# The last tile pair of a down projection: two tiles side by side, or one after the other

## The chip, the core and the metric

The kernel runs on one core of a Trainium2 chip. The core has a matrix engine (TensorE; PE in the profile, its weight loads PEld), a vector engine (VectorE, DVE), a scalar engine (ScalarE, ACT), GpSimd (POOL), and SyncE (SP), which here issues transfers. Matmuls write into PSUM, eight banks of 512 f32 columns each; everything else lives in SBUF, which has 128 partitions. The metric is the time of one execution on the device in microseconds (us), less is better.

## The reference

One row block of 2048 tokens with 640 features, x, goes through two branches that a gate mixes:

```
g = sigmoid((x * gate_w).sum(-1))
a = linear_attention(x) @ wo                     # 32 heads of 20, softmax feature maps
b = (gelu(x @ w_gate) * (x @ w_up)) @ w_down     # 640 -> 1728 -> 640
out = g * a + (1 - g) * b
```

Inputs and output are bf16. The change lies in the last step, where `@ w_down` and `@ wo` are computed and mixed, and in the hidden columns that `@ w_down` reads.

## The kernel before

The 2048 tokens are 16 tiles of 128 rows (t = 0 to 15), in four row blocks (b = 0 to 3) of four tiles. The work goes in this order:

- Attention state (to about 81 us): projections, feature maps and the sums over all tokens.
- Gate and up (`gateup`, to about 195 us): for each block b, 14 chunks c of the 1728 hidden columns, in the order 0, 1, 13, 2, ..., 12. A chunk has 128 columns; the last, c = 13, has 64. For a full chunk TensorE makes five matmuls for the gate into one PSUM bank and five for up into another, ScalarE does the Gelu from the first (line 779) and VectorE multiplies it with the second into `hT`, the hidden activations with hidden columns on partitions (line 781). Chunks take turns on the bank pairs (0, 1) and (6, 7), so a chunk's first matmul waits until the chunk two before it has been read. For c = 13, gate and up fit side by side into 128 columns, so five matmuls into one bank do for both; ScalarE does the Gelu of 64 partitions (line 787), and VectorE multiplies twice (line 792), once for each row half r of `hT` (partitions 0 to 63 and 64 to 127). For block 3, `hT` lies in the space of `xT`, the transposed x, whose first three blocks are done with.
- Down (`downs` and `down_pair`, to the end): tiles go in pairs t0, t0 + 1. Each output element is a sum over 14 chunks of `hT` times `wd_sb` and 5 chunks of `goT` (the attention output, already scaled so that one factor serves both branches) times `wo_sb`. `goT` of tiles 2 to 15 comes from `num`, called between the steps of the pairs ahead (line 968; tiles 14 and 15 during the pair of tiles 12 and 13); it ends in a transposing transfer that SP issues (line 869).

`down_pair` works with matmuls that use 64 of the 128 rows, so that two run side by side, one in each row half, into two banks. A pair is cut into parts h, by output columns: (320, 320), and (256, 256, 128) for the last pair (line 965). In part h, bank `banks[h][j]` holds the columns of tile t0 + j. In the opening, row half r works on bank r: 19 steps of two matmuls (13 full chunks, the half chunk 13, and 5 of `wo_sb`). In the closing, the row halves change banks: 18 steps, because the half chunk has only 64 rows and is needed once for each bank. So in chunk 13 row half r only meets tiles of parity r, and line 792 computes just these: `odd` picks two of the block's four tiles, 64x256 elements for each half.

All parts open first, hidden chunks of every part and then `wo_sb` of every part; then the parts close one after the other. When a part has closed, `evac` multiplies its two banks by the gate's factor into `outsb`: on ScalarE (line 911), and in the last pair the second bank on VectorE (line 909). In the last pair each part's columns of both tiles are then sent to the output in a transfer of their own (line 922); in other pairs there is one transfer at the end. `finish` lets SP wait for all engines and transfers; that is the end of the program.

The helper `_Sched.op` puts a wait in front of an instruction for every earlier one that it depends on (a bank's last reader, a tile's writer). An engine takes its instructions strictly in the order in which the code issues them.

Of the kernel before, what the change touches and what calls it, by code (L numbers as in the profile page):

```python
# [3 lines left out]
P = 128  # L4
# [103 lines left out]
class _Kernel:  # L108
    S, D, H, DH, F = 2048, 640, 32, 20, 1728
    KD = D // P  # L110
# [4 lines left out]
    NFC = 14  # L115
# [644 lines left out]
    def gateup(self, b, c, banks):  # L760
        sc = self.sc
        xs = lambda kt: self.xT[:, kt, b * self.BT:(b + 1) * self.BT]
        xr = [("xT", t) for t in range(4 * b, 4 * b + 4)]
        old = (self.oldw, self.oldk, self.oldq, [("xT", t) for t in range(12)])[b]
        hT, hk = self.hT(b, c), b
        slot = self.gn % 3
        self.gn += 1
        if c < 13:
            i = 0 if c < 7 else 1
            early = c in self.UP + self.LATE  # L770
            done = early and b == 0
            if done:
                banks = banks[::-1]
            for w, wk, bk in ((self.wg_sb, "wg", banks[0]), (self.wu_sb, "wu", banks[1]))[:1 if done else 2]:
                for kt in range(self.KD):
                    key = self.upheld(c)[1] if early and wk == "wu" else (wk, i, kt)
                    self.mm(bk, 0, 512, w[:, kt, c * P:(c + 1) * P], xs(kt), kt == 0, kt == self.KD - 1, xr + [key])
            up, upk = (self.upheld(c)[0], ("upf", c)) if done else (self.bank(banks[1]), ("ps", banks[1]))
            sc.op("act", lambda e: e.activation(self.gl[:, slot, :], self.bank(banks[0]), AF.Gelu_apprx_tanh),  # L779
                  reads=[("ps", banks[0])], writes=[("gl", slot)], guard=self.oldw)  # L780
            sc.op("dve", lambda e: e.tensor_tensor(hT, up, self.gl[:, slot, :], ALU.mult),  # L781
                  reads=[upk, ("gl", slot)], writes=[("hT", hk, c)], guard=old)
        else:
            bk = banks[0]
            for kt in range(self.KD):
                self.mm(bk, 0, 512, self.wgu_sb[:, kt, :], xs(kt), kt == 0, kt == self.KD - 1, xr + ["wgu0", "wgu1"])
            sc.op("act", lambda e: e.activation(self.gl[64:128, slot, :], self.ps[0:64, bk * 512:bk * 512 + 512],
                                                AF.Gelu_apprx_tanh),
                  reads=[("ps", bk)], writes=[("gl", slot)], guard=self.oldw)
            for r in (0, 1):  # L790
                odd = lambda v: v.rearrange("p (u r q) -> p u r q", r=2, q=P)[:, :, r, :]
                sc.op("dve", lambda e: e.tensor_tensor(
                    odd(hT[64 * r:64 * r + 64, :]), odd(self.ps[64:128, bk * 512:bk * 512 + 512]),
                    odd(self.gl[64:128, slot, :]), ALU.mult),
                    reads=[("ps", bk), ("gl", slot)], writes=[("hT", hk, c, r)], guard=old)
# [78 lines left out]
                f()  # L874
        return [lambda p=p: run(p) for p in (small, wide, fin)]

    def down_pair(self, t0, banks, widths):

        sc = self.sc
        ts = (t0, t0 + 1)  # L880
        NFC, KD = self.NFC - 1, self.KD
        nw = len(widths)
        hk = t0 // 4
        last = t0 + 2 == self.NT
        os_ = t0 % 4

        def mm(r, j, h, c, opens, x, n):
            t = ts[j]
            tt, gs, bk, w0, a = t % 4, t % 8, banks[h][j], sum(widths[:h]), 64 * r
            w, end = widths[h], x == n - 1  # L890
            if c <= NFC:
                lhs, rhs = self.hT(hk, c)[a:a + 64, tt * P:(tt + 1) * P], self.wd_sb[a:a + 64, c, w0:w0 + w]
                rd = [("hT", hk, c), "wd"] if c < NFC else [("hT", hk, 13, r), ("wd13", r)]
            else:
                k = c - NFC - 1
                lhs, rhs = self.goT[a:a + 64, gs, k, :], self.wo_sb[a:a + 64, k, w0:w0 + w]
                rd = [("goT", gs), "wo"]
            sc.op("pe", lambda e: e.matmul(self.bank(bk, w), lhs, rhs, start=opens and x == 0, stop=end and not opens,  # L898
                                           skip_group_check=True),
                  reads=rd, writes=[("ps", bk)] + ([("turn", bk)] if end else []), signal=end,  # L900
                  after=[("turn", bk)] if x == 0 and not opens else ())

        def evac(h):
            w0, w = sum(widths[:h]), widths[h]
            for j in (0, 1):
                bk, dst, g = banks[h][j], self.outsb[:, os_ + j, w0:w0 + w], self.Gm[:, ts[j]:ts[j] + 1]
                rd, wr = [("ps", bk), "Gm"], [("outsb", os_ + j, h)]
                if last and j == 1:
                    sc.op("dve", lambda e: e.tensor_scalar(dst, self.bank(bk, w), g, None, op0=ALU.mult), reads=rd, writes=wr)
                else:  # L910
                    sc.op("act", lambda e: e.activation(dst, self.bank(bk, w), AF.Copy, scale=g), reads=rd, writes=wr)  # L911
            if last:
                hs, c0, c1 = [h], w0, w0 + w
            elif h == nw - 1:
                hs, c0, c1 = range(nw), 0, self.D
            else:
                return
            if t0 < self.TB:
                rows = self.out[0:self.BT, :].rearrange("(p j) n -> p j n", j=self.TB)[:, t0:t0 + 2, :]
            else:  # L920
                rows = self.out[t0 * P:(t0 + 2) * P, :].rearrange("(j p) n -> p j n", p=P)
            sc.dma("sp", lambda e: e.dma_start(rows[:, :, c0:c1], self.outsb[:, os_:os_ + 2, c0:c1]),
                   reads=[("outsb", os_ + j, k) for j in (0, 1) for k in hs], writes=[("out", t0, h)])

        wos = [NFC + 1 + k for k in range(KD)]
        opening = list(range(NFC + 1)) + wos
        for part in (range(NFC + 1), range(NFC + 1, len(opening))):
            for h in range(nw):
                for x in part:
                    for r in (0, 1):  # L930
                        mm(r, r, h, opening[x], True, x, len(opening))
                    yield None
        closing = list(range(NFC)) + wos
        for h in range(nw):
            for x, c in enumerate(closing):
                for r in (0, 1):
                    mm(r, 1 - r, h, c, False, x, len(closing))
                if c == closing[-1]:
                    evac(h)
                yield None  # L940
# [8 lines left out]
    def ffn(self):  # L949
        self.gn = 0  # L950
        self.pn = 0
        pairs = [(0, 1), (6, 7)]

        def gateups(b, after, other={}):
            for idx, c in enumerate([0, 1, 13] + list(range(2, 13))):
                self.gateup(b, c, other.get(idx, pairs[self.pn % 2]))
                self.pn += 1
                after(idx)

        def downs(b, side):  # L960
            p = [pairs[(self.pn + k) % 2] for k in (0, 1)]
            n = 0
            for t in (4 * b, 4 * b + 2):
                final = t + 2 == self.NT
                for _ in self.down_pair(t, p + [(2, 3)] if final else p, (256, 256, 128) if final else (320, 320)):
                    n += 1
                    if n in side:
                        self.num(side[n])

        def state(idx):  # L970
            if idx < 4:
                self.gram(12 + idx)
            if idx == 3:
                self.kv_state()
                self.gates()

        left = []

        def first_nums(idx):
            if idx == 4:  # L980
                left.extend(f for steps in self.num_pair() for f in steps)
            for _ in range({4: 1, 5: 1, 6: 2, 7: 1, 8: 1}.get(idx, 0)):
                left.pop(0)()

        def none(idx):
            pass
        at = (1, 31, 61, 91)
        gateups(0, state)
        gateups(1, first_nums, {k: ((0, 1), (0, 1), (0, 5), (1, 2))[k - 5 if k < 7 else 2 + (k - 7) % 2]
                                for k in range(5, 14)})  # L990
        gateups(2, none)
        gateups(3, none)
        for b in range(self.NB):
            downs(b, {at[k]: 4 * b + 2 + k for k in range(4 if b < 3 else 2)})
# [44 lines left out]
```

## Time and profile before

| what | us |
|---|---|
| three runs | 283.30, 283.51, 283.77 (median 283.51) |
| span of the profiled execution, first to last instruction | 282.4 |
| TensorE busy / VectorE / ScalarE | 278.6 / 173.2 / 105.9 |
| attention state, 0 to 81.3: TensorE busy | 79.6 |
| gate and up, 81.3 to 194.8: TensorE busy | 113.5 |
| down without the last pair, 194.8 to 270.0: TensorE busy | 75.2 |
| last pair, 270.0 to 280.3: TensorE busy | 10.3 |
| after the last matmul, 280.3 to 282.4: TensorE busy | 0 |

The granted clock of TensorE is 1.00 in all of these stretches. "Busy" counts a matmul from its start to its modelled end; matmuls overlap in the pipeline, so the pace of a row of matmuls is read from the start of one group to the start of the next, not from the length of a single one. In the timeline a row gives the start, the length, the engine, the line, what is written and read, the shape, and in brackets the idle time before it and what ended that. A matmul's shape is rows used * weight columns, then rows x columns that stream through.

### The profile page before, as it was taken

What the parts mean: (1) busy time and instruction counts of PE and PEld (TensorE: products, weight loads), DVE (VectorE), ACT (ScalarE), POOL (GpSimd) and SP (SyncE); (2) the same over time, 40 slices, a digit from 0 to 9 for tenths busy, and PEclk for the clock granted to TensorE, in tenths of its full rate; (3) what the DMA queues carried; (4) which work ended last, traced back from release to release, by engine and by line L of the source; (5) the groups of instructions that cost most, each with busy time, mean ns of one, the idle gap of its engine ahead of it and who ended that gap; (6) DMA issues with size and microseconds to landing.
All of it is one profiled execution on the core that took longest, in us unless ns stands there. A gap on an engine that the chain in (4) does not pass through costs nothing.

```text
span 282.4 us, 6904 instructions
## 1 busy us (share of the span) xinstructions
PE 278.6 (99%) x2926; PEld 168.6 (60%) x2926; DVE 173.2 (61%) x329; ACT 105.9 (38%) x204; POOL 15.1 (5%) x69
## 2 busy tenths in 40 slices
PE   7999999999999999999999999999999999999996
PEld 4566766665665444444444444445777777777786
DVE  1456999999997523694333324235883883883801
ACT  3246978777793332223232232321112112112011
POOL 7511001101000000000000000000000000000000
PEclk9999999999999999999999999999999999999999
DMA  7999169787789910011000000000133132532221
GB/s 213 193 223 190 29 127 172 153 175 149 157 175 274 350 51 0 2 24 23 2 0 0 0 2 0 0 0 2 26 50 98 46 49 78 66 49 73 73 72 49
DMA packets 60378, 24.11 MB, mean 85 GB/s; under 512 B 51002, under 2 KB 59834, under 8 KB 60346
## 3 DMA queue, kind: packets, MB, share of 16 engines
q1 hardware_dynamic: 59680, 23.63, 38.9%
q8 instruction: 23, 0.38, 0.6%
q10 hardware_dynamic: 666, 0.03, 0.2%
q14 instruction: 9, 0.07, 0.1%
HBM read 9.04 MB, written 2.62 MB: 41 GB/s over the span
## 4 chain that ended last, share of the span: by engine, by line
PE 97%; DMA 1%; SPq 0%; ACT 0%; issue 0%
PE ps L464 58%; PE ps L898 29%; PE ps L599 4%; PE ps L817 2%; PE ps L478 2%; PE ps L637 2%; DMA w<-in_A_wqkv_dram 1%; PE ps L404 1%; SPq L230 0%; SPq L251 0%; ACT outsb L911 0%; PE ps L370 0%
## 5 line engine op out<-in xcount | busy, mean ns | idle before, releaser
L464 PE MATMUL ps<-xT,wu_sb 128*128 128x512 bf16 x260 | 64.1, 379 | 0.0
L464 PE MATMUL ps<-xT,wg_sb 128*128 128x512 bf16 x260 | 63.9, 379 | 0.0
L779 ACT ACTIVATE gl<-ps 128x512 bf16<-128x512 f32 x52 | 31.0, 597 | 70.3 <-PE ps L464 70.3
L464 PE MATMUL ps<-w,xT 128*128 128x362 bf16 (+5 forms) x340 | 51.4, 302 | 0.0
L898 PE MATMUL ps<-wd_sb,hT 64*128 64x320 bf16 x648 | 48.4, 296 | 0.0
L781 DVE TENSOR_TENSOR hT<-ps,gl 128x512 bf16<-128x512 f32 x34 | 23.4, 689 | 37.7 <-PE ps L464 37.7
L464 PEld LDWEIGHTS ps<-xT,wu_sb 128*128 128x128 bf16 x260 | 25.4, 98 | 30.3 <-DVE hT L781 0.2
L464 PEld LDWEIGHTS ps<-xT,wg_sb 128*128 128x128 bf16 x260 | 25.1, 98 | 29.8 <-issue 0.2
L911 ACT ACTIVATE outsb<-ps,Gm 128x320 bf16<-128x320 f32 (+2 forms) x31 | 14.5, 515 | 71.8 <-PE ps L898 71.8
L464 PEld LDWEIGHTS ps<-w,xT 128*128 128x128 bf16 x340 | 31.9, 97 | 14.8
L898 PEld LDWEIGHTS ps<-wd_sb,hT 64*128 64x128 bf16 x648 | 30.9, 94 | 12.2 <-issue 0.4
L898 PE MATMUL ps<-wo_sb,goT 64*128 64x320 bf16 (+2 forms) x340 | 26.5, 288 | 0.0
L617 DVE TENSOR_REDUCE Dk<-Ek 128x66 f32<-128x1320 bf16 x16 | 24.3, 1520 | 2.3 <-ACT gcol L528 2.3
L626 DVE TENSOR_TENSOR Ek<-Ek,Dk 128x1320 bf16<-128x1320 bf16 x16 | 24.5, 1532 | 0.5
L863 DVE TENSOR_TENSOR O<-ps,RH 128x640 bf16<-128x640 f32 x32 | 24.7, 815 | 0.0
L538 ACT ACTIVATE Ek<-ps 128x627 bf16<-128x627 f32 x32 | 20.5, 693 | 6.4 <-PE ps L599 4.9
L538 ACT ACTIVATE Eqt<-ps 128x627 bf16<-128x627 f32 x32 | 20.6, 705 | 2.5 <-PE ps L464 2.5
L781 DVE TENSOR_TENSOR xT<-ps,gl 128x512 bf16<-128x512 f32 x13 | 9.0, 690 | 18.2 <-PE ps L464 18.2
L898 PEld LDWEIGHTS ps<-wo_sb,goT 64*128 64x128 bf16 x340 | 15.9, 94 | 5.3
L898 PE MATMUL ps<-wd_sb,xT 64*128 64x320 bf16 (+2 forms) x270 | 16.0, 269 | 0.0
L851 DVE RECIPROCAL RH<-ps 128x32 f32<-128x32 f32 x16 | 5.7, 357 | 14.4 <-PE ps L817 14.3
L898 PEld LDWEIGHTS ps<-wd_sb,xT 64*128 64x128 bf16 x270 | 12.1, 94 | 2.7
(90 smaller groups left out, 184.1 us busy)
## 6 DMA issues: line engine op xcount, KB each, us to landing
out_dram<-outsb SPq DMA_DIRECT2D x7, 320.0 KB, 2.3
wd_sb<-in_B_w_down_dram SPq DMA_DIRECT2D x1, 2080.0 KB, 11.0
wg_sb<-in_B_w_gate_dram SPq DMA_DIRECT2D x5, 224.0 KB, 3.1
wg_sb<-in_B_w_gate_dram SPq DMA_DIRECT2D x5, 192.0 KB, 3.5
wu_sb<-in_B_w_up_dram SPq DMA_DIRECT2D x5, 192.0 KB, 3.9
wo_sb<-in_A_wo_dram SPq DMA_DIRECT2D x1, 800.0 KB, 9.7
xtok<-in_A_x_dram SPq DMA_DIRECT2D x2, 320.0 KB, 3.3
w<-in_A_wqkv_dram SPq DMA_DIRECT2D x4, 160.0 KB, 4.0
```

The source lines that it names most:

```text
L464: self.sc.op("pe", lambda e: e.matmul(self.ps[:, bank * 512 + c0:bank * 512 + c0 + n], lhs, rhs, start=first, stop=fin), reads=reads, writ ...
L478: sc.op("pe", lambda e, c0=c0, n=n, bk=bk, col=col: e.matmul(self.bank(bk)[:, col:col + n], self.xT[:, kt, t * P:(t + 1) * P], self.w3[:, ...
L538: self.sc.op("act", lambda e: e.activation(dst, src, AF.Exp, scale=scale), reads=[("ps", b), ("ps", b + 1)], writes=[(name, sl, s)])
L599: self.sc.op("pe", lambda e: e.matmul(out, self.xT[:, kt, t * P:(t + 1) * P], self.w3[:, kt, c:c + 2 * n].rearrange("p (r w) -> p r w", w= ...
L617: self.sc.op("dve", lambda e: e.tensor_reduce(self.Dk[:, se, 0, :].rearrange("p (u h) -> p u h", h=self.HG), self.k_view(se), AX.X, ALU.ad ...
L626: sc.op("dve", lambda e: e.tensor_tensor(v, v, R.rearrange("p (u h) -> p u h", h=self.HG).unsqueeze(3).to_broadcast([P, 2 * self.G, self.H ...
L779: sc.op("act", lambda e: e.activation(self.gl[:, slot, :], self.bank(banks[0]), AF.Gelu_apprx_tanh), reads=[("ps", banks[0])], writes=[("g ...
L781: sc.op("dve", lambda e: e.tensor_tensor(hT, up, self.gl[:, slot, :], ALU.mult), reads=[upk, ("gl", slot)], writes=[("hT", hk, c)], guard=old)
L851: dve(lambda e: e.reciprocal(R(0), Dn[1]), rb, [key(0)], guard=old)
L863: dve(lambda e, o=o, f=f, s=s: e.tensor_tensor(o, V[s][:, :, 0:DH], f, ALU.mult), rb + [key(6 + s)], [("O", s, sl)], guard=old)
L898: sc.op("pe", lambda e: e.matmul(self.bank(bk, w), lhs, rhs, start=opens and x == 0, stop=end and not opens, skip_group_check=True), reads ...
L911: sc.op("act", lambda e: e.activation(dst, self.bank(bk, w), AF.Copy, scale=g), reads=rd, writes=wr)
```

## The change

In the last pair both row halves work on columns of the same tile. Part 0 is tile 14: columns 0 to 319 in one bank, 320 to 639 in the other. Part 1 is tile 15, columns 0 to 223 and 224 to 447; part 2 is tile 15, columns 448 to 543 and 544 to 639. The number of matmuls and the columns that they stream in all are the same. Each part goes out in one transfer of one tile: 640, 448 and 192 columns in 128 rows, where there were 256, 256 and 128 columns of two tiles in 256 rows. As each row half now meets both tiles with chunk 13, line 792 computes, for block 3, all four tiles in each row half: two multiplies of 64x512. The other pairs and blocks are as they were.

```diff
@@ -788,7 +788,7 @@
                                                 AF.Gelu_apprx_tanh),
                   reads=[("ps", bk)], writes=[("gl", slot)], guard=self.oldw)
             for r in (0, 1):
-                odd = lambda v: v.rearrange("p (u r q) -> p u r q", r=2, q=P)[:, :, r, :]
+                odd = lambda v: v if b == 3 else v.rearrange("p (u r q) -> p u r q", r=2, q=P)[:, :, r, :]
                 sc.op("dve", lambda e: e.tensor_tensor(
                     odd(hT[64 * r:64 * r + 64, :]), odd(self.ps[64:128, bk * 512:bk * 512 + 512]),
                     odd(self.gl[64:128, slot, :]), ALU.mult),
@@ -874,20 +874,22 @@
                 f()
         return [lambda p=p: run(p) for p in (small, wide, fin)]
 
-    def down_pair(self, t0, banks, widths):
+    def down_pair(self, t0, banks, last):
 
         sc = self.sc
-        ts = (t0, t0 + 1)
-        NFC, KD = self.NFC - 1, self.KD
-        nw = len(widths)
+        NFC, KD, D = self.NFC - 1, self.KD, self.D
         hk = t0 // 4
-        last = t0 + 2 == self.NT
-        os_ = t0 % 4
+        if last:
+            parts = [((t0, 0, 320), (t0, 320, 320)), ((t0 + 1, 0, 224), (t0 + 1, 224, 224)),
+                     ((t0 + 1, 448, 96), (t0 + 1, 544, 96))]
+        else:
+            parts = [((t0, c, 320), (t0 + 1, c, 320)) for c in (0, 320)]
+        nw = len(parts)
 
         def mm(r, j, h, c, opens, x, n):
-            t = ts[j]
-            tt, gs, bk, w0, a = t % 4, t % 8, banks[h][j], sum(widths[:h]), 64 * r
-            w, end = widths[h], x == n - 1
+            t, w0, w = parts[h][j]
+            tt, gs, bk, a = t % 4, t % 8, banks[h][j], 64 * r
+            end = x == n - 1
             if c <= NFC:
                 lhs, rhs = self.hT(hk, c)[a:a + 64, tt * P:(tt + 1) * P], self.wd_sb[a:a + 64, c, w0:w0 + w]
                 rd = [("hT", hk, c), "wd"] if c < NFC else [("hT", hk, 13, r), ("wd13", r)]
@@ -901,26 +903,27 @@
                   after=[("turn", bk)] if x == 0 and not opens else ())
 
         def evac(h):
-            w0, w = sum(widths[:h]), widths[h]
             for j in (0, 1):
-                bk, dst, g = banks[h][j], self.outsb[:, os_ + j, w0:w0 + w], self.Gm[:, ts[j]:ts[j] + 1]
-                rd, wr = [("ps", bk), "Gm"], [("outsb", os_ + j, h)]
+                t, w0, w = parts[h][j]
+                bk, dst, g = banks[h][j], self.outsb[:, t % 4, w0:w0 + w], self.Gm[:, t:t + 1]
+                rd, wr = [("ps", bk), "Gm"], [("outsb", t % 4, h, j)]
                 if last and j == 1:
                     sc.op("dve", lambda e: e.tensor_scalar(dst, self.bank(bk, w), g, None, op0=ALU.mult), reads=rd, writes=wr)
                 else:
                     sc.op("act", lambda e: e.activation(dst, self.bank(bk, w), AF.Copy, scale=g), reads=rd, writes=wr)
+            os_ = t0 % 4
             if last:
-                hs, c0, c1 = [h], w0, w0 + w
+                c1 = w0 + w
+                c0 = parts[h][0][1]
+                sc.dma("sp", lambda e: e.dma_start(self.out[t * P:(t + 1) * P, c0:c1], self.outsb[:, t % 4, c0:c1]),
+                       reads=[("outsb", t % 4, h, j) for j in (0, 1)], writes=[("out", t0, h)])
             elif h == nw - 1:
-                hs, c0, c1 = range(nw), 0, self.D
-            else:
-                return
-            if t0 < self.TB:
-                rows = self.out[0:self.BT, :].rearrange("(p j) n -> p j n", j=self.TB)[:, t0:t0 + 2, :]
-            else:
-                rows = self.out[t0 * P:(t0 + 2) * P, :].rearrange("(j p) n -> p j n", p=P)
-            sc.dma("sp", lambda e: e.dma_start(rows[:, :, c0:c1], self.outsb[:, os_:os_ + 2, c0:c1]),
-                   reads=[("outsb", os_ + j, k) for j in (0, 1) for k in hs], writes=[("out", t0, h)])
+                if t0 < self.TB:
+                    rows = self.out[0:self.BT, :].rearrange("(p j) n -> p j n", j=self.TB)[:, t0:t0 + 2, :]
+                else:
+                    rows = self.out[t0 * P:(t0 + 2) * P, :].rearrange("(j p) n -> p j n", p=P)
+                sc.dma("sp", lambda e: e.dma_start(rows[:, :, :], self.outsb[:, os_:os_ + 2, :]),
+                       reads=[("outsb", os_ + j, k, j) for j in (0, 1) for k in range(nw)], writes=[("out", t0, h)])
 
         wos = [NFC + 1 + k for k in range(KD)]
         opening = list(range(NFC + 1)) + wos
@@ -962,7 +965,7 @@
             n = 0
             for t in (4 * b, 4 * b + 2):
                 final = t + 2 == self.NT
-                for _ in self.down_pair(t, p + [(2, 3)] if final else p, (256, 256, 128) if final else (320, 320)):
+                for _ in self.down_pair(t, p + [(2, 3)] if final else p, final):
                     n += 1
                     if n in side:
                         self.num(side[n])
```

## The prediction

> **What bounds the kernel now.** I read the page's busy table and chain of waits first, then the timeline of the last 12 us, then the timeline of the one other place that the diff touches.
>
> ```profile
> PE 278.6 (99%) x2926; PEld 168.6 (60%) x2926; DVE 173.2 (61%) x329; ACT 105.9 (38%) x204; POOL 15.1 (5%) x69
> ...
> PE 97%; DMA 1%; SPq 0%; ACT 0%; issue 0%
> PE ps L464 58%; PE ps L898 29%; PE ps L599 4%; PE ps L817 2%; PE ps L478 2%; PE ps L637 2%; DMA w<-in_A_wqkv_dram 1%; PE ps L404 1%; SPq L230 0%; SPq L251 0%; ACT outsb L911 0%; PE ps L370 0%
> ```
>
> TensorE is busy 99% of the span and the chain is TensorE for 97%. So a column more or less on TensorE, a wait put in front of it, and the tail behind its last matmul count; nothing else does. The end, from the timeline (start, length, engine, line):
>
> ```profile
> 265.10 1.93 PE L898 MATMUL ps<-wd_sb,xT 64*128 64x320 bf16 x26
> 266.87 0.84 PE L898 MATMUL ps<-wo_sb,goT 64*128 64x320 bf16 x10
> ...
> 271.25 9.88 SPq L922 DMA_DIRECT2D out_dram<-outsb  x4
> ...
> 275.20 1.58 PE L898 MATMUL ps<-wd_sb,xT 64*128 64x256 bf16 x26
> 276.62 0.71 PE L898 MATMUL ps<-wo_sb,goT 64*128 64x256 bf16 x10
> ...
> 279.13 0.89 PE L898 MATMUL ps<-wd_sb,xT 64*128 64x128 bf16 x26
> 279.33 0.48 DVE L909 TENSOR_SCALAR outsb<-ps,Gm 128x256 bf16<-128x256 f32 x1 [1.48 <-PE ps L898]
> 279.86 0.44 PE L898 MATMUL ps<-wo_sb,goT 64*128 64x128 bf16 x10
> 280.37 0.37 ACT L911 ACTIVATE outsb<-ps,Gm 128x128 bf16<-128x128 f32 x1 [0.53 <-PE ps L898]
> ```
>
> The last matmul ends at 279.86 + 0.44 = 280.30; the last evacuation runs from 280.37 to 280.74; the last issue ends at 271.25 + 9.88 = 281.13, and an issue takes 0.37, so it began at 280.76; its transfer lands 1.6 later (its row is shown below), at 282.4, the end of the span. The runs' median, 283.51, lies 1.1 us above this span, and I carry that 1.1 over unchanged.
>
> The other place is the half chunk c = 13 of the last row block, whose two multiplies (line 792) the first hunk of the diff touches:
>
> ```profile
> 170.96 1.24 PE L464 MATMUL ps<-xT,wg_sb 128*128 128x512 bf16 x5
> 171.16 0.59 ACT L787 ACTIVATE gl<-ps 64x512 bf16<-64x512 f32 x1 [1.56 <-PE ps L464]
> 171.85 0.89 DVE L792 TENSOR_TENSOR xT<-ps,gl 64x256 bf16<-64x256 f32 x2 [1.08 <-ACT gl L787]
> 172.04 1.24 PE L464 MATMUL ps<-xT,wu_sb 128*128 128x512 bf16 x5
> 172.91 0.53 PEld L464 LDWEIGHTS ps<-xT,wg_sb 128*128 128x128 bf16 x3
> 173.12 0.59 PE L464 MATMUL ps<-xT,wg_sb 128*128 128x512 bf16 x2
> ```
>
> Chunk 13 has five matmuls and one bank, and only the ten matmuls of c = 2 (170.96 to 173.12) stand between it and c = 3, whose first matmul writes that same bank. VectorE lets go of it at 171.85 + 0.89 = 172.74, and c = 3's first weights load at 172.91: a slack of 0.17 us.
>
> **1. The two wider multiplies at c = 13.** Each row half now needs chunk 13 for all four tiles of the block, so each multiply is 64x512 in place of 64x256. The same kind of operation by shape:
>
> ```profile
> L792 DVE TENSOR_TENSOR xT<-ps,gl x2: 426/428/429, 171.9 to 172.3; 64x256 bf16<-64x256 f32 x2
> ...
> L781 DVE TENSOR_TENSOR xT<-ps,gl x13: 690/690/691, 167.9 to 194.9; 128x512 bf16<-128x512 f32 x13
> ```
>
> Twice the columns cost 0.262 us more. That the partition count doesn't matter I take from ScalarE, where a 64x512 Gelu takes 0.59 (above) and a 128x512 one 0.60 (597 ns on the page). So 0.69 each. They end at 171.85 + 2 x 0.69 + 0.03 (the gap in 0.89 = 2 x 0.428 + 0.03) = 173.26, which is after the 172.91 at which TensorE wants the bank. Its restart: VectorE, idle, began 0.10 after the Gelu ended (171.75 to 171.85), which I take for the release; and from weights to matmul an idle TensorE needs 0.03, as after the gap at 81.27:
>
> ```profile
> 81.27 0.34 PEld L464 LDWEIGHTS ps<-xT,wg_sb 128*128 128x128 bf16 x3 [0.19 <-issue]
> 81.30 0.59 PE L464 MATMUL ps<-xT,wg_sb 128*128 128x512 bf16 x2
> ```
>
> c = 3 then starts at 173.39 in place of 173.12: **+0.27 us**. Behind it in TensorE's queue stands everything that is left, back to back, so nothing gives the stall back. ScalarE and VectorE have about 1.5 us idle ahead of each Gelu and multiply (the 1.56 above), so they only shift along; c = 2's own multiply (173.32 before) finds VectorE free at 173.26. Bounds: at 0.43 a multiply (if the columns cost nothing) there is no stall; at 0.86 (twice the narrow one) they end at 173.60 and the stall is 0.61. A restart of 0.17 + 0.21 (the unstalled distances above) in place of 0.13 gives 0.52.
>
> **2. TensorE in the last pair.** Instructions: three parts, each with 19 opening and 18 closing steps of two matmuls, before and after. Per part, columns go from 256, 256, 128 to 320, 224, 96: the sum stays 640. What can change is the price of a narrow step. Two row halves run side by side; a step of two by start-to-start times: 320 wide (266.87 - 265.10) / 13 = 136 ns; 256 wide (276.62 - 275.20) / 13 = 109 ns; 128 wide (279.86 - 279.13) / 13 = 56 ns; 66 wide, from line 817's matmuls, which also go in row halves:
>
> ```profile
> 263.81 0.50 PE L817 MATMUL ps<-KV,Eq 64*128 64x66 bf16 x22
> 264.15 1.11 PE L898 MATMUL ps<-wo_sb,goT 64*128 64x320 bf16 x14
> ```
>
> (264.15 - 263.81) / 11 = 31 ns. Between these lines, 224 costs 96 and 96 costs 43. New sum 136 + 96 + 43 = 275 ns, old 109 + 109 + 56 = 274; times 37 steps, **+0.04 us**, which is nothing. Bounds: by strict proportion from 128 the 96-wide step is 42 (no gain); if it can't go below the 128-wide 56 ns, it costs 37 x 13 = 0.48 us more. Row 817 at 31 ns speaks for the first.
>
> [...]
>
> Waits: the second part's opening starts later (14 x 136 in place of 14 x 109 ns after the first), which gives the banks it waits for more time; the order of weights, goT and closing is unchanged, and the two goT transposes are issued before the pair begins.
>
> **3. The tail.** The last evacuation is 96 wide in place of 128. ScalarE takes 0.367 for 128 and 0.473 for 256, so 0.83 ns a column: **-0.03**. The last transfer is 48 KB in 128 rows in place of 64 KB in 256:
>
> ```profile
> out_dram<-outsb SPq DMA_DIRECT2D x7, 320.0 KB, 2.3
> ...
> out_dram<-outsb SPq DMA_DIRECT2D x2, 128.0 KB, 1.8
> ...
> out_dram<-outsb SPq DMA_DIRECT2D x1, 64.0 KB, 1.6
> ```
>
> Bytes: (1.8 - 1.6) / 64 x 16 = 0.05 less. Rows: tile pair 2 and 3, also 320 KB but in 128 rows, lands in 2.2 where the 256-row ones take 2.3: 0.1 less. Together -0.15; bounds 0 (landing is a fixed time) and -0.2. I take **-0.12**. The cover for the transfer before it: the second part's evacuation (224 wide, 0.45) starts 18 x 43 = 0.77 before the last matmul's end, so SP has issued that transfer 0.03 + 0.45 + 0.05 + 0.37 = 0.90 after that start, while the last evacuation ends at 0.77 + 0.03 + 0.34 = 1.14. SP keeps 0.24 to spare; without it the end would move by the same amount.
>
> Sum: 0.27 + 0.04 - 0.03 - 0.12 = +0.16, so **283.7 us** on the median, a change of 0.06%. About 0.2% (0.57 us) is what a measurement of this kernel can tell from no change: its runs span 283.30 to 283.77.
>
> **The rivals.**
> A, the forecast: a short stall and a shorter tail that nearly cancel, 283.7. For it: 0.69 against a slack of 0.17. Chance 0.50.
> B, no stall: VectorE treats the now contiguous 64x512 faster, or the release comes in time. Only step 3 is left, 283.51 - 0.15 = 283.4. Against it: all 47 rows of line 781 that read PSUM, contiguous ones, take 0.68 to 0.69. Chance 0.17.
> C, the 96-wide steps are held at the 128-wide pace: +0.16 + 0.44 = 284.1, slower. The place is the third part, opening and closing; it decides from a step above 55 ns. Against it: row 817. Chance 0.11.
> D, the last transfer gets no shorter (its landing is a fixed time, so the parts don't do what they say at the end): +0.28, 283.8. Against it: the three landing times above. Chance 0.12.
> E, the stall is at its upper bound, 0.61, and more where TensorE's weights refill late: 283.51 + 0.61 - 0.11 = 284.0, slower by 0.18%; it passes 284.08 only with D. Chance 0.07.
> Faster by over 0.57 us needs something that no row shows: 0.03.
>
> **How the numbers follow.** Within 0.2% lie A, B, D and most of E; slower is C's better half and a part of E, plus the spread of the runs (0.24 either way around the median): 0.15. Faster, with B's lower end and the spread, 0.06; so 0.79 within. The range 283.2 to 284.1 takes B's 283.4 less 0.2 at one end and C's and E's 284.0 to 284.1 at the other.
>
> **What would show it.** Step 1: in the profile after, line 792 has 64x512 at 0.69 and TensorE shows a gap of about 0.3 us ahead of c = 3, near 173.1, with VectorE named as the releaser; wrong if c = 3 still starts 2.16 us after c = 2. Step 2: 37 steps of the third part at 43 ns; C if at 56. Step 3: the last transfer lands about 1.5 us after its issue, and SP is free before the last evacuation ends. A change beyond 0.6 us either way would make the whole account wrong.

## The result, and the profile after

The changed kernel takes 284.07 us (median of 10 runs, 283.52 to 284.62) where the kernel before, run beside it, takes 283.32 (283.04 to 283.78): a ratio of 1.0022, 95% interval 1.0012 to 1.0032. By the ratio that is +0.62 us, and 0.34 to 0.91 by its interval; the two medians lie 0.75 apart. The forecast was +0.16 with a range of 283.2 to 284.1: the time lies in the range, 0.03 below its upper end, and the sign is right, but the size is nearly four times what was forecast and lies just on the far side of the 0.2% that I had called "within". It also just passes the 0.6 us that the prediction named as the sign that its whole account is wrong; what of the account failed is worked out below.

Before and after can't be compared by absolute times alone, because the start of the program varies from execution to execution (c = 13 of block 3 starts at 169.89 in the profile before, at 169.57 after, though nothing ahead of it was changed). So I measure from that chunk's first matmul, in two lengths:

| profiled execution | c = 13 to the last matmul's end | from there to the end of the program (the tail) | together |
|---|---|---|---|
| before | 110.41 | 2.14 | 112.55 |
| after | 110.71 | 2.60 | 113.31 |
| difference | +0.30 | +0.46 | +0.76 |

The page of the changed kernel, its busy table and its chain of waits by engine and by line:

```profile
PE 277.9 (98%) x2912; PEld 168.0 (59%) x2926; DVE 173.8 (61%) x329; ACT 106.0 (37%) x204; POOL 15.2 (5%) x69
...
PE 96%; DMA 1%; DVE 0%; issue 0%; SPq 0%; ACT 0%; DVEq 0%
PE ps L464 57%; PE ps L900 29%; PE ps L599 4%; PE ps L817 2%; PE ps L478 2%; PE ps L637 2%; DMA w<-in_A_wqkv_dram 1%; PE ps L404 1%; DVE xT L792 0%; SPq L230 0%; ACT gl L787 0%; SPq L251 0%; ACT outsb L913 0%; PE ps L370 0%; DVEq L42 0%
```

TensorE still makes up the chain, but the two multiplies of line 792 and the Gelu of line 787 ahead of them are on it now, which they were not before. (The view infers this chain; for another execution of the changed kernel, e7 below, with the same stall, it leaves them out. The times below are the firmer sign.)

The first term, in the timeline of the changed kernel around c = 13 (start, length, engine, line; in brackets the idle time and what ended it):

```profile
170.85 0.59 ACT L787 ACTIVATE gl<-ps 64x512 bf16<-64x512 f32 x1 [1.56 <-PE ps L464]
171.54 1.42 DVE L792 TENSOR_TENSOR xT<-ps,gl 64x512 bf16<-64x512 f32 x2 [1.08 <-ACT gl L787]
171.73 1.24 PE L464 MATMUL ps<-xT,wu_sb 128*128 128x512 bf16 x5
...
173.08 0.77 PEld L464 LDWEIGHTS ps<-xT,wg_sb 128*128 128x128 bf16 x5 [0.60 <-ACT gl L779]
173.11 1.24 PE L464 MATMUL ps<-xT,wg_sb 128*128 128x512 bf16 x5
```

The two multiplies now end at 171.54 + 1.42 = 172.96; c = 3's weights load 0.12 later and its matmuls start at 173.11. c = 2's last five matmuls start at 171.73; before, c = 3 followed such a start by 173.12 - 172.04 = 1.08, now by 1.38: a stall of 0.30. The view names the Gelu of c = 2 as what ended this wait; but that was done at 172.53. TensorE's queue holds a second wait ahead of this load, for VectorE, and the trace has that one ending at 173.05, 0.09 after the second multiply.

The second term, in the timeline of the end, and in the rows of issues of the transfers view:

```profile
279.35 0.72 PE L900 MATMUL ps<-wd_sb,xT 64*128 64x96 bf16 x26
...
279.90 0.38 PE L900 MATMUL ps<-wo_sb,goT 64*128 64x96 bf16 x10
280.08 1.32 SPq L918 DMA_DIRECT2D out_dram<-outsb  x2
280.32 0.32 DVE L911 TENSOR_SCALAR outsb<-ps,Gm 128x96 bf16<-128x96 f32 x1 [0.32 <-PE ps L900]
280.35 0.34 ACT L913 ACTIVATE outsb<-ps,Gm 128x96 bf16<-128x96 f32 x1 [0.32 <-PE ps L900]
```

```profile
q1 hardware_dynamic: 432, 0.33, 17.1%
q8 instruction: 1, 0.02, 1.6%
issues: line engine op xcount, KB each, median us to landing
out_dram<-outsb SPq DMA_DIRECT2D x1, 160.0 KB, 3.9
out_dram<-outsb SPq DMA_DIRECT2D x1, 112.0 KB, 2.6
out_dram<-outsb SPq DMA_DIRECT2D x1, 48.0 KB, 2.1
```

The 96-wide steps run at (279.90 - 279.35) / 13 = 42 ns, and the last matmul ends at 280.28, 10.31 after the pair's first, as before (269.99 to 280.30). But SP's last issue takes 0.68 (280.72 to 281.40) in place of 0.37, and all three transfers land late: part 0, with half the bytes of a usual pair, takes 3.9 us where a usual pair takes 2.3, and the last takes 2.1 with 48 KB where 64 KB took 1.6. The row above the issues, in the stretch from 278 to 284, is new to this account: one instruction transfer. It holds 1.6% of 16 engines for 6 us, that is 1.5 us on one of them. The trace's packet records put it at 279.53 to 281.02: a single packet of 16 KB. The trace has 16 increments of a semaphore for the landing of each of the three transfers, as many as the page counts DMA engines; I take one increment for one engine's share, 8 of 128 packets. Part 0's transfer has 15 of them by 280.27, and the sixteenth at 282.33. Of its 128 packets 120 are done by 279.90; the last eight, by that reading one DMA engine's share, start only at 281.01, as the fetch ends. The trace doesn't name the engine of a packet; that the fetch and these eight share one is read from these times. (The profile after lacks 14 of the 2926 matmul records; that changes no reading here.)

### The profile page after: what moved, and what is told of

It reads as the page before. It is cut to its first block, busy times and chain, and to the rows that moved or that the text cites. A ratio compares the mean times of both kernels' runs of the same rounds, so it can differ in the third digit from the quotient of the medians.

```text
span 282.9 us, 6888 instructions
## 1 busy us (share of the span) xinstructions
PE 277.9 (98%) x2912; PEld 168.0 (59%) x2926; DVE 173.8 (61%) x329; ACT 106.0 (37%) x204; POOL 15.2 (5%) x69
## 4 chain that ended last, share of the span: by engine, by line
PE 96%; DMA 1%; DVE 0%; issue 0%; SPq 0%; ACT 0%; DVEq 0%
PE ps L464 57%; PE ps L900 29%; PE ps L599 4%; PE ps L817 2%; PE ps L478 2%; PE ps L637 2%; DMA w<-in_A_wqkv_dram 1%; PE ps L404 1%; DVE xT L792 0%; SPq L230 0%; ACT gl L787 0%; SPq L251 0%; ACT outsb L913 0%; PE ps L370 0%; DVEq L42 0%
## 5 line engine op out<-in xcount | busy, mean ns | idle before, releaser
L464 PE MATMUL ps<-xT,wu_sb 128*128 128x512 bf16 x256 | 63.2, 379 | 0.3
L464 PE MATMUL ps<-xT,wg_sb 128*128 128x512 bf16 x250 | 61.8, 379 | 0.7 <-issue 0.2
```

Of the source, the lines that this page charges most:

```text
L464: self.sc.op("pe", lambda e: e.matmul(self.ps[:, bank * 512 + c0:bank * 512 + c0 + n], lhs, rhs, start=first, stop=fin), reads=reads, writ ...
```

## The experiments

Two theories had to be told apart from rivals: S, the stall at c = 13, 0.30 us that nothing gives back; and F, that the last 16 KB fetch of TensorE's instructions holds one DMA engine while part 0's transfer is on it, so that what follows on that engine is late. Ratios are to the kernel before, run on the same chip beside them.

**e1, the wider multiplies alone**, in the kernel before:

```diff
-                odd = lambda v: v.rearrange("p (u r q) -> p u r q", r=2, q=P)[:, :, r, :]
+                odd = lambda v: v if b == 3 else v.rearrange("p (u r q) -> p u r q", r=2, q=P)[:, :, r, :]
```

> The kernel before with only the wider multiplies at c = 13 of block 3 (the extra half is computed and never read). Theory S (stall): TensorE starts c = 3 of block 3 about 0.30 us late, as it did after the change (431 to 432 ns between two starts where a missing record lies, 515 there), and the time is 0.30 us (0.1%) above before; the tail stays as before, with the last transfer landing 1.6 us after its issue. Rival (all of the loss lies in the tail): the gap is given back later, and the time is that of before within 0.1 us.

Measured: 1.0012 (0.9998 to 1.0026), that is +0.34 us, with no change just inside the interval. The profile is sharper: from c = 13 to the last matmul 110.71 (+0.30), tail 2.14 (as before). Its timeline:

```profile
171.51 1.42 DVE L792 TENSOR_TENSOR xT<-ps,gl 64x512 bf16<-64x512 f32 x2 [1.08 <-ACT gl L787]
171.70 1.24 PE L464 MATMUL ps<-xT,wu_sb 128*128 128x512 bf16 x5
...
173.08 1.24 PE L464 MATMUL ps<-xT,wg_sb 128*128 128x512 bf16 x5
```

The same 1.38 between the two starts, from this edit alone. S stands, and the stall is not given back later.

**e2, c = 13 of block 3 in a bank of its own**, in the changed kernel:

```diff
-        gateups(3, none)
+        gateups(3, none, {2: (2, 3)})
```

> The changed kernel with c = 13 of block 3 in bank 2, which nobody uses in that stage, so that c = 3 need not wait for the two multiplies. Theory S: the 0.30 us stall is gone and the time falls by 0.3 us against the changed kernel, to about 0.4 us above before; the last transfer still lands 2 us or more after its issue in most executions. Rival: another wait takes its place (bank 2 is first used again in the down phase), no gain.

Measured: 1.0014 (0.9999 to 1.0028), against 1.0022 for the changed kernel. The two intervals overlap, so the times alone don't show the expected 0.3; the profile does. In it c = 13 to the last matmul is 110.41, exactly as before, with the same 1.42 us of multiplies (c = 3 starts 1.08 after c = 2's last five matmuls again); no other wait took the stall's place. The tail stays at 2.57. This time the fetch came later (279.76 to 281.00), missed part 0 (1.9) and met part 1:

```profile
out_dram<-outsb SPq DMA_DIRECT2D x1, 160.0 KB, 1.9
out_dram<-outsb SPq DMA_DIRECT2D x1, 112.0 KB, 2.4
out_dram<-outsb SPq DMA_DIRECT2D x1, 48.0 KB, 2.1
```

**e3 and e4, the fetch moved out of the way.** The trace has 23 fetches of 16 KB, on average one every 127 matmuls with their weight loads, so I take them for fetches of TensorE's instructions, at about a fixed place in its stream: in the profiles before and after, each of the 23 begins after the same number of weight loads to within 21, the last after 2900 and after 2902 of the 2926. With 56 more matmuls in the warm-up it falls earlier (in e3 it ended 3.35 us ahead of the last issue, in the changed kernel 0.31 after that issue had begun); e3 is the changed kernel, e4 the kernel before with the same edit:

```diff
-        for n in (512, 512, 512, 512, 512, 512, 128, 128, 128):
+        for n in (512, 512, 128, 128, 128):
...
+        for i in range(60):
+            a, b = ((0, 2), (64, 3))[i % 2]
+            sc.op("pe", lambda e: e.matmul(self.bank(b, 16), ones[a:a + 64, 0:P], ones[a:a + 64, 0:16], start=True, stop=True),
+                  writes=[("ps", b)], signal=i >= 60 - 2)
```

> The changed kernel with 56 more matmuls in TensorE's warm-up (60 matmuls of 16 columns in place of 4 of 512), so that the last 16 KB instruction fetch, which comes at a fixed place in TensorE's instruction stream, falls some 2.5 us earlier, about 277 us, ahead of the first of the last three transfers. Theory F (the fetch holds one DMA engine, and the packets of part 0's transfer on that engine wait behind it, and part 1's and 2's behind those): the last transfer lands 1.5 us after its issue, the issue takes 0.35 and not 0.68, and the time is 0.4 to 0.5 us below the changed kernel, 0.2 above before, with a smaller spread from run to run. Rival R (128-row transfers, or issues 0.64 us apart, are slow themselves): the last landing stays near 2.1, the time does not fall.

> Control for the same 56 warm-up matmuls: the kernel before with them. Theory F: before, the fetch at 279.34 falls between the transfers of part 0 (packets to 279.39) and part 1 (from 280.76), so moving it changes nothing: within 0.1 us of before. If the warm-up itself costs or saves time at the start, it shows here and is taken off the third run.

Measured: the warm-up isn't free. e3 is at 1.0043 (1.0027 to 1.0060), e4 at 1.0041 (1.0025 to 1.0057), so my expectations of their times missed by about 1 us, and e3's runs don't spread less than the changed kernel's either. The two against each other differ by 0.06 us where the changed kernel without the edit stood 0.62 above before, but each interval is 0.9 us wide, so these times alone decide nothing. The profiles, measured from c = 13, leave the start out: e3 takes 110.71 + 1.97 = 112.68, 0.63 less than the changed kernel, and e4 110.42 + 2.14 = 112.55, as before to 0.01 us. In e3 the stretch from 278 to 284 has no instruction row, and the three transfers:

```profile
q1 hardware_dynamic: 432, 0.33, 16.9%
issues: line engine op xcount, KB each, median us to landing
out_dram<-outsb SPq DMA_DIRECT2D x1, 160.0 KB, 1.8
out_dram<-outsb SPq DMA_DIRECT2D x1, 112.0 KB, 1.7
out_dram<-outsb SPq DMA_DIRECT2D x1, 48.0 KB, 1.5
```

The same three transfers, issued the same 0.64 us apart, now land in 1.8, 1.7 and 1.5. The last two issues, which took 1.32 together, take 0.97:

```profile
280.60 0.97 SPq L922 DMA_DIRECT2D out_dram<-outsb  x2
```

So the last issue takes 0.33 in place of 0.68. Rival R, that 128-row transfers close together are slow themselves, falls. The tail is 0.17 shorter than before's, a little more than the prediction had claimed for the narrower last part (0.03 + 0.12).

**e5 to e9, the fetch moved by less, at no cost.** The same warm-up columns in 27 pieces, 18 matmuls more:

```diff
-        for n in (512, 512, 512, 512, 512, 512, 128, 128, 128):
+        for n in (128,) * 27:
```

e5 is the changed kernel with it; e6 and e9 add e2's spare bank; e7 is the changed kernel unedited; e8 the kernel before with the split warm-up.

> The changed kernel with its warm-up of six 512-wide and three 128-wide matmuls cut into 27 of 128, the same columns, so 18 more matmuls at (about) no more time; the last fetch comes 18 matmuls earlier, about 279.0 in place of 279.5, with part 0's transfer still on the engines from 279.3 to 279.85. Theory F with a backlog that needs time to drain: part 0's transfer still lands late on one engine (about 3 us after its issue or more), but that engine is free again by about 280.5 and has drained before the last transfer, which lands 1.5 us after its issue; from c = 13's first matmul to the end of the program it takes 112.7 us (before 112.55, changed 113.31), and the time is 0.4 to 0.6 below the changed kernel's. Rival F2 (any collision of the fetch with one of these transfers costs the end its full length): the end stays at 113.2 or more.

> Both: c = 13 of block 3 in bank 2, and the warm-up cut into 27. Theories S and F: no stall, a free tail; from c = 13's first matmul to the end 112.4 us, 0.15 below before; time 0.1 to 0.2 below before, which this measurement can hardly tell from the same. If the tail collides after all, 112.8 to 113.0.

> The changed kernel again, beside the other two on the same chip: 284.0 to 284.2, 0.6 to 0.75 above before; in the profile the last transfer lands 2 us or more after its issue where the last fetch ends after 280.9, and about 1.5 to 1.7 where it ends earlier (in 4 of its 10 runs the span was 282.3 to 282.4, which I take for short fetches).

> The kernel before with only the warm-up cut into 27 matmuls of 128 columns. If the gain of the kernel with spare bank and cut warm-up over before (0.9991) came from the tail alone, this one is the same as before (within 0.1 us), and from c = 13's first matmul to the end it takes 112.55 us. If the cut warm-up itself saves time at the start, this one is faster than before too, by about 0.1 us, and the tail's share of the gain is what is left: 0.16.

> The changed kernel with c = 13 of block 3 in bank 2 and the warm-up cut into 27, again, beside the one above: 0.16 us below it, 0.1 to 0.3 below before; from c = 13's first matmul to the end 112.39 us.

| | ratio, 95% interval | c = 13 to last matmul | tail | together |
|---|---|---|---|---|
| e5, split warm-up | 1.0006, 0.9997 to 1.0015 | 110.71 | 1.97 | 112.68 |
| e6, spare bank and split | 0.9991, 0.9983 to 1.0000 | 110.42 | 1.97 | 112.39 |
| e9, the same again | 0.9998, 0.9988 to 1.0007 | 110.42 | 1.97 | 112.38 |
| e7, changed, again | 1.0028, 1.0017 to 1.0039 | 110.71 | 2.68 | 113.39 |
| e8, before, split warm-up | 0.9997, 0.9988 to 1.0006 | 110.42 | 2.14 | 112.55 |

e7 repeats the late end: its fetch ends at 281.05 and its last transfer lands 2.20 after its issue, as expected; its median, 284.24, is just above the expected 284.2.

e5 is the most telling. By the runs it lies 0.62 us below e7, the changed kernel beside it, and their intervals don't overlap; e8 shows that the split warm-up by itself gains nothing. In its profile the fetch (278.20 to 279.33) still met part 0's transfer, which lands late (2.5, where I had expected 3 or more), yet the end is free:

```profile
q8 instruction: 1, 0.02, 1.2%
issues: line engine op xcount, KB each, median us to landing
out_dram<-outsb SPq DMA_DIRECT2D x1, 160.0 KB, 2.5
out_dram<-outsb SPq DMA_DIRECT2D x1, 112.0 KB, 1.7
out_dram<-outsb SPq DMA_DIRECT2D x1, 48.0 KB, 1.5
```

So F2, that any meeting costs the end its full length, falls too: here a fetch that ended 1.03 us ahead of the last issue left the last landing at 1.49 after its issue, as in e3. e1 shows the same in the layout before: its first part took 3.6 us by the semaphore records (the fetch ran from 279.29 to 280.29), and its last still landed in 1.6. What sets the late ends apart, in all eleven profiles, is when the fetch ends, against the moment at which SP begins to issue the last transfer:

| | fetch ends, against the last issue's start | last issue takes | last landing after its start | tail |
|---|---|---|---|---|
| e3 | 3.35 before | 0.33 | 1.49 | 1.97 |
| e5 | 1.03 before | 0.33 | 1.49 | 1.97 |
| e6 | 0.53 before | 0.33 | 1.49 | 1.97 |
| e1 | 0.41 before | 0.37 | 1.63 | 2.14 |
| before | 0.34 before | 0.37 | 1.63 | 2.14 |
| after | 0.31 after | 0.68 | 2.12 | 2.60 |
| e7 | 0.38 after | 0.74 | 2.20 | 2.68 |
| e2 | 0.56 after | 0.93 | 2.10 | 2.57 |

(e4, e8 and e9 are free ones too, at 3.72, 1.49 and 1.00 before. No profile lies between 0.34 before and 0.31 after, so the limit itself isn't measured.) In the three bad rows SP's last issue ends 0.37 us after the fetch does (0.68 - 0.31, 0.74 - 0.38, 0.93 - 0.56), little more than the 0.33 that this issue takes in the free rows of e3, e5 and e6: this fits SP being held until the fetch has ended. What holds it isn't shown, and not every issue during a fetch is held: the second of the three began inside the fetch in before, e1, e2, after and e7, and took 0.34 to 0.37. In after the engine then still has all eight of its packets of part 0 to move (281.01 to 281.82), and in after and e7 the last transfer lands 1.44 and 1.46 after its issue has ended where the free ones need 1.16; in e2, where only part 1 was behind the fetch, 1.17.

The version of e6 and e9 removes both losses in the profile, at 112.39 and 112.38. Its two ratios, 0.9991 and 0.9998, and e8's 0.9997 without the change can't be told from each other: the 0.17 us that the profiles show is under what these runs resolve, since the start of the program alone varies by more. So e9's expected 0.16 below e8 shows in the profiles and not in the times.

## Why the prediction was right or wrong

Step 1 was right: 0.69 forecast and 0.694 measured for each multiply, a stall of 0.27 forecast and 0.30 measured, shown by e1 alone and by its removal in e2. The release and restart came out as 0.15 (172.96 to 173.11) where I had 0.13. Rival B (no stall) and E (0.61) fall.

Step 2 was right: 136, 96 and 43 ns forecast for the three parts, and 136, 95 and 42 measured; the pair takes as long as before (269.97 to 280.28 after, 269.99 to 280.30 before). Rival C falls: a pair of 96-wide matmuls takes 42 ns, where a pair of 128-wide ones took 56 before.

Step 3 is the one that failed: "The last transfer is 48 KB in 128 rows in place of 64 KB in 256 ... I take -0.12". With the engines free this is right (1.49 in place of 1.63, and 0.03 from the evacuation: a tail of 1.97 in e3, e5, e6). In the changed kernel the tail came out 0.46 longer than before in place of 0.15 shorter: -0.17 from the narrower part, and 0.63 from the fetch (2.60 against 1.97). "SP keeps 0.24 to spare" held as far as it went, since SP was done with the second issue 0.27 before the last evacuation ended, but it looked at SP's own queue only. What I left out, the DMA engines themselves, stood in the trace before (276 to 284):

```profile
q1 hardware_dynamic: 816, 0.33, 15.4%
q8 instruction: 1, 0.02, 0.8%
```

By the packet records this instruction fetch ran from 279.34 to 280.41, between part 0's packets (the last ends at 279.39) and part 1's (from 280.76). It ended only 0.34 ahead of the last issue, so before was not far from the same collision. The change closes part 0 half a microsecond later, because a 320-wide closing takes 18 x 136 ns where a 256-wide took 18 x 109; its packets, which ran from 278.82 to 279.39 before, run from 279.31 on, while the fetch, which goes with TensorE's stream (after 2900 of the 2926 weight loads before, 2902 after), starts at 279.53 and so falls among them. Rival D had the right place, a tail that doesn't get shorter, but gave it no more than a return to 1.6; a longer one was not among my cases. So the mechanism was right for +0.31 of the sum (0.27 + 0.04, measured +0.30) and wrong for the tail, by 0.61. That the time still lay in the range is luck: its upper end, 284.1, was there for C and E, neither of which happened, and nothing in the working allowed for a longer tail.

In the ten runs of the changed kernel the span goes from 282.3 to 283.4. That the short ones are those whose fetch ended early would fit the table above, but only profiled executions show the fetch, so it isn't shown; and in the 25 runs of before beside e7 the span varies by nearly as much (281.7 to 282.7), with the start of the program.

## What to carry to other kernels

Ahead of moving work to the end of a kernel, look at everything that uses the DMA engines there, the instruction rows too, and not just at the queue that issues: here one 16 KB packet held up the transfer that it met (part 0's landed 3.9 us after its issue where it took 1.8 in e3), and where it ended after the last issue had begun, the end came 0.6 to 0.7 us later; where it ended 0.34 us or more ahead of that issue, it cost the end nothing. Two tiles' worth of rows for a half chunk is not free just because VectorE is idle: what counts is the slack until its bank is wanted (0.17 us here, and a stall of 0.30), and a spare bank bought it back (110.41 from c = 13 to the last matmul in e2, as before, in place of 110.71).

## What the runs showed of the hardware

A fetch of 16 KB took 0.88 to 1.82 us in the profiles before and after, always as one packet, on average every 127 matmuls with their weight loads (88 to 159 between two of them before). That they bring TensorE's instructions is read from their place in its stream, since the trace doesn't say whose instructions a packet holds. TensorE itself isn't late for the last of the 23 here (the 96-wide steps run at 42 ns in the profile after, and at 42 in e3, where no fetch is near), but the output transfers are: it costs the end of the program 0.63 us (2.60 against 1.97). What the others cost I didn't measure.

An issue on SP isn't always the 0.33 to 0.37 us that the others took here: with a fetch still running, the last of three took 0.68 to 0.93, and ended 0.37 after the fetch in each of three cases; the second of three, also during the fetch, was not held.

The place of the fetch is only nearly fixed: with the same 18 matmuls added it began 1.72 us ahead of the last matmul's end in e5, 1.04 in e6 and 1.78 in e9; without them 0.75 and 0.80 in the two profiles of the changed kernel, and 0.24 in e2, whose matmuls are the same. So what the fetch meets can differ between executions with the same matmuls: in e2 it missed part 0 and met part 1.
